# A retention recurrence followed by a two-layer MLP on one core: four small changes of order and of loading, made together

## The chip, the core and the metric

The kernel runs on one core of a Trainium2 chip. The core has five engines, each with its own instruction stream and each executing it in order: PE (TensorE, matrix products; its weight loads are shown as PEld), DVE (VectorE), ACT (ScalarE), POOL (GpSimd) and SP (SyncE, which here only issues DMA transfers). An instruction waits on semaphores for what it needs from other engines or from a transfer. The metric is the device time of one execution in microseconds.

## The reference

The first half is a linear-attention recurrence with decay over 768 positions, for 4 batches and 8 heads of width 64. The second half takes its output as 3072 tokens of width 512 and runs them through a two-layer network with a leaky activation.

```python
for t in range(S):                                   # S = 768, D = 64
    state = gamma * state + outer(k[:, :, t], v[:, :, t])
    y[:, :, t] = scale * (q[:, :, t] @ state)
x = y.transpose(0, 2, 1, 3).reshape(3072, 512)
h = x @ w_in                                         # 512 -> 2048
g = max(h, 0) + alpha * min(h, 0)
out = g @ w_out                                      # 2048 -> 512
```

## The kernel before

The tokens are worked in six blocks of 512 (`n` from 0 to 5). A block is four chunks of 128 positions. For each chunk the recurrence is computed in its chunked form: scores of the chunk (`sca`, `scb`), masked by DVE, products with v, and a state carried from chunk to chunk (`sta`, `stb`, `ss`, `t`). The first eight chunks are worked as four units of 256 positions (functions that begin with `u`), the others one by one or in pairs. The results of two chunks stand in two PSUM banks, `ya` and `yb`, one for each half of the rows, and are passed on to the 16-bit tile `xT[n]`, which is the input of the first layer of block `n`. Where part of the result was computed ahead into banks `za`/`zb` and copied to `zs`, passing on means: in one half of the columns of a bank ACT copies (`own`), in the other DVE adds `zs` (`other`). In the kernel before, both work on `ya` first and then on `yb`, and because they read the same bank, ACT's copy waits for DVE's addition (`put_y`, line 606, for chunks; `uout_copy`, line 572, for units).

The first layer is `ffn1_half` (blocks 0 and 1, two output tiles of 256 tokens at a time), `ffn1` (rest of block 0, and block 2) and `ffn1_mix` (blocks 3 to 5). After each output tile ACT makes `hm` and DVE the 16-bit activation `gt`. `ffn1_mix` computes part of the layer with seven products of quarter matrices in place of eight (a Strassen-Winograd form). It needs four sums and differences of quarters of w_in, `wins` 0 to 3 (`win_sum`, made once, on POOL, during block 2), and four of quarters of `xT`, `xsum` 0 to 3 (`x_sum`, two on DVE and two on POOL, for each block).

The second layer is `ffn2` (block 0) and `seven` (blocks 1 to 5), again seven products, of quarters of `gt` and w_out. `seven` needs sums of quarters of `gt`: `g_sums(n, part, which, engine)` makes for half `part` of the groups the sum `which`: 0 is `gs` 0 (sum of two quarters of `gt`), 1 is `gs` 1 (`gs` 0 minus a quarter), 2 is `third`, 3 changes `gt` itself. With `part` None both halves are made by one instruction. The first two products of `seven` use `gt`, the third uses `gs` 1.

Everything is in one written order: the position of a call in the program sets where its instructions stand in the streams of their engines. `tick(gen, m)` issues `m` matrix products of a layer between other calls.

The inputs come in through a ring of twelve 512 KB staging buffers (`ring`), and all loads are issued by SP in order. The first of four column pieces of w_in is loaded by `load_first` as two halves of 256 columns, each with all four row groups `j`; the other pieces by `load_w` as two halves of two row groups each, all 512 columns. POOL and ACT cast them to 16 bits (`cast_first`, `cast_w`).

Of the kernel before, what the change touches and what calls it, by code (L numbers as in the profile page):

```python
# [11 lines left out]
COPY = mybir.ActivationFunctionType.Copy  # L12
# [7 lines left out]
def kernel(  # L20
# [10 lines left out]
    nc = tc.nc  # L31
# [285 lines left out]
    def out_second(us):  # L317
        if us[0] not in zs:
            out_states(us, 1)
        z = zs.pop(us[0], None)  # L320
        yv, _ = ys.pop(us[0])
        nb, at = divmod(us[0], UB)
        if at == 0:
            xT[nb] = sbp.tile([128, 2, NP, TB // 2], F16, tag="xT", bufs=2, name=f"xT{nb}")
        to = xT[nb][:, at // 2].rearrange("p a (t x j) -> p a t x j", x=2, j=64)
        for X in range(2):
            put_y(to[:, :, :, X, :], yv[X], X, z and z[X])

    ustaged, ukq, ukT, uv, um = {}, {}, {}, {}, {}

# [242 lines left out]
    def uout_copy(w, shared=False, z=None):  # L573
        y = uy.pop(w)[0]
        nb, at = divmod(2 * w, UB)
        if at == 0:
            xT[nb] = sbp.tile([128, 2, NP, TB // 2], F16, tag="xT", bufs=2, name=f"xT{nb}")
        for X in range(2):
            lo = C * X
            to = xT[nb][:, at // 2, :, lo : lo + C].rearrange("p a (n j) -> p a j n", j=2)  # L580
            src = y[X].rearrange("p (a j n) -> p a j n", j=2, n=64)
            if z and z[X]:
                own, other = slice(2 * X, 2 * X + 2), slice(2 - 2 * X, 4 - 2 * X)
                nc.vector.tensor_tensor(out=to[:, other], in0=src[:, other], in1=z[X], op=ADD)  # L584
                nc.scalar.activation(
                    out=to[:, own], in_=src[:, own], func=COPY, bias=0.0, scale=1.0
                )
            elif shared and X == 0:
# [14 lines left out]
        nc.scalar.activation(out=t, in_=b[:, 0:256], func=COPY, bias=0.0, scale=1.0)  # L603
        return t

    def put_y(to, src, X, z):
        if z is None:
            nc.scalar.activation(out=to, in_=src, func=COPY, bias=0.0, scale=1.0)
            return
        own, other = slice(2 * X, 2 * X + 2), slice(2 - 2 * X, 4 - 2 * X)  # L610
        nc.vector.tensor_tensor(out=to[:, other], in0=src[:, other], in1=z, op=ADD)
        nc.scalar.activation(out=to[:, own], in_=src[:, own], func=COPY, bias=0.0, scale=1.0)

    gts = {}

# [436 lines left out]
    def load_w(nm, i, parts=2):  # L1052
        n = 4 // parts
        for j in (0, 2):
            t = ring(f"{nm}{i}{j}").rearrange("p (j d) -> p j d", j=2)
            if nm == "wi":
                src = wi[:, j : j + 2, 512 * i : 512 * i + 512]
            else:
                src = wo[:, 4 * i + j : 4 * i + j + 2, :]
            for jj in range(0, 2, n):  # L1060
                nc.sync.dma_start(out=t[:, jj : jj + n], in_=src[:, jj : jj + n])
            for jj in range(2):
                wst[nm, i, j + jj] = t[:, jj]
# [9 lines left out]
                eng.tensor_copy(out=to, in_=t)  # L1073


    def load_first():
        for c in range(2):
            t = ring(f"wi0{c}").rearrange("p (j d) -> p j d", j=4)
            nc.sync.dma_start(out=t, in_=wi[:, :, 256 * c : 256 * c + 256])
            wst["first", c] = t  # L1080

    def cast_first(c, engs):
        t = wst.pop(("first", c))
        for j, eng in zip(range(4), engs):
            to = w_in_all[:, j, 256 * c : 256 * c + 256]
            if eng is nc.scalar:
                eng.activation(out=to, in_=t[:, j], func=COPY, bias=0.0, scale=1.0)
            else:
                eng.tensor_copy(out=to, in_=t[:, j])
# [184 lines left out]
    for n in range(1, NBLK):  # L1274
        more = n + 1 < NBLK
        u0 = UB * (n + 1)
        if n == 2:
# [46 lines left out]
        if more:  # L1324
# [122 lines left out]
```

## Time and profile before

| | |
|---|---|
| median of three runs | 197.99 us (lowest 197.58) |
| the profiled execution's own time | 198.98 us |
| its span, first to last instruction | 197.0 us, so 1.98 us lie around it |
| PE busy | 189.3 us, 96% of the span |
| DVE, ACT, POOL busy | 151.3, 121.7 and 147.5 us |
| granted TensorE clock | 1.0 throughout |
| DMA | 38.78 MB, mean 197 GB/s |

A row of the timeline has the start, the duration, the engine, the line of the kernel, the operation, output<-inputs with the shape, and a count; a bracket at its end names the idle time before it and what ended it. Durations of a single instruction overlap a little with the next one, since engines begin an instruction before the last one has left them. A row of the chain has start, duration and what the chain went through in that time: "SPq" is SP's queue, "DMA" a transfer under way.

### The profile page before, as it was taken

How to read it: one execution, taken by the hardware profiler on the slowest of the kernel's cores; microseconds unless marked ns; L12 is line 12 of the kernel's file. 1: busy time of each engine (PE TensorE's matmuls, PEld its weight loads, DVE VectorE, ACT ScalarE, POOL GpSimd, SP SyncE). 2: the span in 40 equal slices, each digit the busy share in tenths (PEclk: the TensorE clock that was granted, in tenths of full speed). 3: DMA queues.
4: the chain of work that ended last, by engine and by line, in shares of the span. 5: the costliest groups of instructions: out<-in, count | busy, mean ns of one | idle time of the engine just before them, and what ended most of it. 6: DMA issues, size and time to landing. Idle time of an engine off the chain costs nothing.

```text
span 197.0 us, 6461 instructions
## 1 busy us (share of the span) xinstructions
PE 189.3 (96%) x2668; PEld 131.7 (67%) x2668; DVE 151.3 (77%) x260; ACT 121.7 (62%) x272; POOL 147.5 (75%) x148
## 2 busy tenths in 40 slices
PE   7789899999999989999999999999999999999993
PEld 5657444557768878744688754788754888654882
DVE  2597889253999698588897879968879977799943
ACT  3368664349687863476458988749987433687120
POOL 3286788999996955999659999579999397589000
PEclk9999999999999999999999999999999999999999
DMA  6999999999999989899999999993890011200014
GB/s 168 310 336 350 404 396 296 332 358 179 210 230 148 214 257 272 196 215 299 196 231 228 226 185 265 237 221 93 113 263 2 3 57 63 100 3 0 2 57 160
DMA packets 92749, 38.78 MB, mean 197 GB/s; under 512 B 70176, under 2 KB 88624, under 8 KB 92720
## 3 DMA queue, kind: packets, MB, share of 16 engines
q1 hardware_dynamic: 91440, 37.36, 77.2%
q10 hardware_dynamic: 1280, 1.01, 1.5%
q8 instruction: 21, 0.34, 0.7%
q14 instruction: 8, 0.07, 0.1%
HBM read 27.35 MB, written 6.29 MB: 171 GB/s over the span
## 4 chain that ended last, share of the span: by engine, by line
PE 73%; SPq 10%; DMA 7%; POOL 6%; DVE 1%; issue 1%; POOLq 0%
PE ops L809 30%; PE hps L942 16%; PE hps L632 12%; PE hps L972 5%; SPq L340 4%; SPq L117 4%; DMA wi<-in_moe_w_in_dram 4%; PE ops L734 4%; POOL wsum L757 3%; DMA kqs<-in_q_dram 3%; PE ya L293 1%; PE yb L293 1%; POOL gs L757 1%; DVE gs L757 1%; POOL ukq L354 1%; PE sca L234 1%
## 5 line engine op out<-in xcount | busy, mean ns | idle before, releaser
L809 PEld LDWEIGHTS <-gt 128*128 128x128 f16 x320 | 30.6, 98 | 4.2
L942 PE MATMUL hps<-xT,win 128*128 128x512 f16 x144 | 33.0, 379 | 0.0
L929 DVE SCALAR_TENSOR_TENSOR gt<-hm,small,hps 128x512 f16<-128x512 f32 (+1 forms) x42 | 28.7, 706 | 5.1 <-ACT hm L925 3.8
L809 PE MATMUL ops<-wout,gt 128*128 128x256 f16 x240 | 28.4, 273 | 0.0
L925 ACT ACTIVATE hm<-hps 128x512 f32<-128x512 f32 x39 | 23.1, 593 | 6.1 <-PE hps L942 5.4
L632 PE MATMUL hps<-xT,win 128*128 128x512 f16 x112 | 24.7, 379 | 0.6 <-POOL win L1073 0.6
L137 POOL TENSOR_TENSOR kq<-kqs,tab 128x512 f16<-128x512 f32 x23 | 23.7, 1051 | 1.9 <-DMA kqs<-in_q_dram 1.9
L642 DVE SCALAR_TENSOR_TENSOR gt<-hm,small,hps 128x512 f16<-128x512 f32 x28 | 20.9, 748 | 3.8 <-ACT hm L641 0.9
L942 PEld LDWEIGHTS <-win 128*128 128x128 f16 x144 | 14.1, 98 | 14.5
L641 ACT ACTIVATE hm<-hps 128x512 f32<-128x512 f32 x28 | 16.7, 597 | 8.9 <-PE hps L632 8.6
L674 DVE SCALAR_TENSOR_TENSOR gt<-hm,small,hps 128x256 f16<-128x256 f32 x40 | 16.9, 476 | 5.0 <-ACT hm L669 5.0
L827 ACT ACTIVATE kept<-ops 128x512 f32<-128x512 f32 x15 | 9.0, 597 | 18.8 <-PE ops L809 18.7
L632 PEld LDWEIGHTS <-win 128*128 128x128 f16 x112 | 10.9, 98 | 13.6 <-POOL win L1073 1.1
L809 PE MATMUL ops<-wsum,gs 128*128 128x256 f16 x160 | 19.0, 273 | 0.7 <-DVE gs L757 0.7
L217 POOL TENSOR_TENSOR t<-ss,tab 128x256 f16<-128x256 f32 x13 | 8.7, 669 | 13.6 <-DVE ss L215 13.6
L757 POOL TENSOR_TENSOR gt<-gt,gs 128x1024 f16<-128x1024 f16 x8 | 17.0, 2126 | 2.2 <-DVE gs L757 2.2
L660 PE MATMUL hps<-xT,win 128*128 128x256 f16 x160 | 18.4, 273 | 0.0
L129 ACT ACTIVATE kq<-kqs,tab 128x64 f16<-128x64 f32 x72 | 18.0, 336 | 0.0
L660 PEld LDWEIGHTS <-win 128*128 128x128 f16 x160 | 15.4, 98 | 2.6 <-DVE xT L584 0.3
L809 PEld LDWEIGHTS <-gs 128*128 128x128 f16 x160 | 15.1, 98 | 3.0 <-DVE gs L757 1.0
L669 ACT ACTIVATE hm<-hps 128x512 f32<-128x512 f32 x20 | 11.8, 597 | 4.5 <-PE hps L660 4.4
L839 DVE TENSOR_TENSOR os<-ops,kept 128x512 f32<-128x512 f32 (+1 forms) x17 | 10.5, 624 | 5.0 <-ACT kept L827 3.7
(139 smaller groups left out, 391.5 us busy)
## 6 DMA issues: line engine op xcount, KB each, us to landing
out_dram<-os SPq DMA_DIRECT2D x20, 256.0 KB, 3.6
wi<-in_moe_w_in_dram SPq DMA_DIRECT2D x8, 512.0 KB, 8.6
wo<-in_moe_w_out_dram SPq DMA_DIRECT2D x8, 512.0 KB, 8.7
kqs<-in_k_dram SPq DMA_DIRECT2D x16, 256.0 KB, 4.4
kqs<-in_q_dram SPq DMA_DIRECT2D x16, 256.0 KB, 4.3
vs<-in_v_dram SPq DMA_DIRECT2D x16, 256.0 KB, 4.7
ku<-in_k_dram SPq DMA_DIRECT2D x4, 256.0 KB, 4.4
qu<-in_q_dram SPq DMA_DIRECT2D x4, 256.0 KB, 5.3
```

Source lines behind the costliest of these rows:

```text
L129: eng.activation(out=kqs[u][:, a, h % 4, h // 4, :], in_=staged[u][nm][:, h, :], func=COPY, bias=0.0, scale=tab[:, H * a + h : H * a + h + 1],
L137: eng.tensor_tensor(out=kqs[u][:, a].rearrange("p i r d -> p r i d"), in0=staged[u][nm].rearrange("p (r i) d -> p r i d", i=4), in1=tab[:, ...
L632: nc.tensor.matmul(out=hps, lhsT=w_in_all[:, hp, 128 * ft : 128 * ft + 128], rhs=xT[n][:, :, hp, :], start=(hp == 0), stop=(hp == 3),)
L641: nc.scalar.activation(out=hm, in_=hps, func=RELU, bias=0.0, scale=-1.0)
L642: nc.vector.scalar_tensor_tensor(out=gt_at(n, ft, slice(0, TB)), in0=hm, scalar=oma_sb[:, ft : ft + 1], in1=hps, op0=MULT, op1=ADD,)
L660: nc.tensor.matmul(out=hps[:, 256 * (ft - f0) : 256 * (ft - f0) + 256], lhsT=w_in_all[:, hp, 128 * ft : 128 * ft + 128], rhs=xT[n][:, half ...
L674: nc.vector.scalar_tensor_tensor(out=gt_at(n, f, to), in0=hm[:, at], scalar=oma_sb[:, f : f + 1], in1=hps[:, at], op0=MULT, op1=ADD,)
L757: eng.tensor_tensor(out=out, in0=a, in1=b, op=op)
L809: nc.tensor.matmul(out=bk[:, 256 * t : 256 * t + 256], lhsT=a[:, f, 128 * t : 128 * t + 128], rhs=w[:, f, :], start=first and f == 0 and ( ...
L925: nc.scalar.activation(out=t, in_=src, func=RELU, bias=0.0, scale=-1.0)
L929: nc.vector.scalar_tensor_tensor(out=gt_at(n, f, cols), in0=hm, scalar=oma_sb[:, f : f + 1], in1=src, op0=MULT, op1=ADD,)
L942: nc.tensor.matmul(out=hps, lhsT=w_in_all[:, hp, 128 * ft : 128 * ft + 128], rhs=x[:, :, hp, :], start=(hp == 0), stop=(hp == 3),)
```

## The change

Four edits, made together.

1. The second piece of w_in (columns 512 to 1023) is loaded and cast like the first: as two halves of 256 columns with all four row groups (`load_columns(1)`, `cast_columns(2)` and `(3)`). POOL casts six tiles of 256 columns in place of three of 512. ACT casts two of 256 in place of one of 512, the second of them after the first output tile of `ffn1(0, lo=4)`.
2. Passing on (`put_crossed`): DVE begins on `ya` as before and ACT on `yb`; then they change banks.
3. In block 1 the three group sums on DVE are made in the order (1, 0), (0, 1), (1, 1) in place of (0, 1), (1, 0), (1, 1).
4. `win_sum(3)` on POOL moves from the end of block 2's first layer to after the `x_sum` calls for block 3.

```diff
+        put = [(to[:, :, :, X, :], yv[X]) for X in range(2)]
+        if z:
+            put_crossed(put, z)
+            return
...
+    def put_crossed(put, z):
+        own, other = [slice(0, 2), slice(2, 4)], [slice(2, 4), slice(0, 2)]
+
+        def add(X):
+            to, src = [a[:, other[X]] for a in put[X]]
+            nc.vector.tensor_tensor(out=to, in0=src, in1=z[X], op=ADD)
+
+        def copy(X, at):
+            to, src = [a[:, at] for a in put[X]]
             nc.scalar.activation(out=to, in_=src, func=COPY, bias=0.0, scale=1.0)
...
+        if z[0] is not None:
+            add(0)
+        copy(1, own[1])
+        copy(0, slice(0, 4) if z[0] is None else own[0])
+        add(1)
...
-    load_first()
-    load_w("wi", 1)
+    load_columns(0)
+    load_columns(1)
     load_w("wi", 2)
...
-    cast_first(0, [A, G, G, G])
-    cast_first(1, [A, G, A, G])
-    cast_w("wi", 1, [G, G, G])
+    cast_columns(0, [A, G, G, G])
+    cast_columns(1, [A, G, A, G])
+    cast_columns(2, [G, G, G])
+    cast_columns(3, [G, G, G])
...
             if half and f:
-                cast_w("wi", 1, [A])
+                cast_columns(2, [A], [3])
...
-    for _ in ffn1(0, lo=4):
+    gen = ffn1(0, lo=4)
+    tick(gen, 4)
+    cast_columns(3, [A], [3])
+    for _ in gen:
         pass
...
-            for i in range(4):
+            for i in range(3):
                 win_sum(i, G)
...
-            ((0, 1), (1, 0), (1, 1)) if n == 1 else ((None, 0), (None, 1)) if more else ((1, 0), (1, 1))
+            ((1, 0), (0, 1), (1, 1)) if n == 1 else ((None, 0), (None, 1)) if more else ((1, 0), (1, 1))
...
                 x_sum(n + 1, 3, G)
+                if n == 2:
+                    win_sum(3, G)
```

DVE's instructions around block 1's group sums, before. The `gs` row with `gt` alone is sum (1, 0); the two with `gs` and `gt` are (0, 1) and (1, 1); sum (0, 0) is made by POOL.

```order
L674 SCALAR_TENSOR_TENSOR gt_992<-hm,small,hps 128x256 x18
L757 TENSOR_TENSOR gs_1356<-gs_1355,gt_992 128x1024
L757 TENSOR_TENSOR gs_1355<-gt_992 128x1024
L757 TENSOR_TENSOR gs_1356<-gs_1355,gt_992 128x1024
L839 TENSOR_TENSOR os<-ops,kept 128x512
```

The same place now (the edit has moved the line numbers):

```order
L686 SCALAR_TENSOR_TENSOR gt_996<-hm,small,hps 128x256 x18
L769 TENSOR_TENSOR gs_1359<-gt_996 128x1024
L769 TENSOR_TENSOR gs_1360<-gs_1359,gt_996 128x1024 x2
L851 TENSOR_TENSOR os<-ops,kept 128x512
L203 TENSOR_TENSOR t_8_1542<-ut_4_1054,sta 128x256
```

Sum (1, 0) now stands right behind the last activation of the first layer, and the two that make `gs` 1 follow it.

POOL's instructions from the end of block 2 into block 3's first layer, before (`t` is the decayed state, `kq` a scaled k or q, `hm` and `gt` the end of a Winograd part):

```order
L217 TENSOR_TENSOR t_16_2413<-ss_2411,tab 128x256
L757 TENSOR_TENSOR xsum<-xT_2358 128x512
L757 TENSOR_TENSOR xsum<-xT_2358,xsum 128x512
L137 TENSOR_TENSOR kq_2566<-kqs_2019,tab 128x2x4x64 x2
L1002 TENSOR_TENSOR hm<-hm,small 128x512
L1008 TENSOR_TENSOR gt_2597<-hm,kept 128x2x256
```

The same place now:

```order
L217 TENSOR_TENSOR t_16_2416<-ss_2414,tab 128x256
L769 TENSOR_TENSOR xsum<-xT_2361 128x512
L769 TENSOR_TENSOR xsum<-xT_2361,xsum 128x512
L769 TENSOR_TENSOR wins<-win,wins 128x512
L137 TENSOR_TENSOR kq_2570<-kqs_2023,tab 128x2x4x64 x2
L1014 TENSOR_TENSOR hm<-hm,small 128x512
L1020 TENSOR_TENSOR gt_2601<-hm,kept 128x2x256
```

`wins` 3 stands between `xsum` 3 and the two `kq`; in front of the `t` rows of block 2 it is gone.

ACT's instructions at the end of block 2's recurrence, before:

```order
L603 ACTIVATE zs<-za 128x256
L603 ACTIVATE zs<-zb 128x256
L612 ACTIVATE xT_2358<-ya 128x4x64
L612 ACTIVATE xT_2358<-yb 128x4x64
L129 ACTIVATE kq_2389<-kqs_2014,tab 128x64 x8
L985 ACTIVATE kept<-hps 128x512
```

The same place now:

```order
L606 ACTIVATE zs<-za 128x256
L606 ACTIVATE zs<-zb 128x256
L618 ACTIVATE xT_2361<-yb 128x4x64
L618 ACTIVATE xT_2361<-ya 128x4x64
L129 ACTIVATE kq_2392<-kqs_2018,tab 128x64 x8
L997 ACTIVATE kept<-hps 128x512
```

The two copies have changed places; `kept` is the copy that frees a bank for the next Winograd part. The copy from `yb` waits for PE alone, the copy from `ya` for DVE's addition on `ya`, and DVE's addition on `yb` for ACT's copy from `yb`. The streams of PE hold the same products in the same order, and SP's the same transfers but for the shape of the two of edit 1.

More of the change, by code (lines that the diff above doesn't have):

```diff
@@ L325, in out_second @@
         to = xT[nb][:, at // 2].rearrange("p a (t x j) -> p a t x j", x=2, j=64)
-        for X in range(2):
-            put_y(to[:, :, :, X, :], yv[X], X, z and z[X])
+        put = [(to[:, :, :, X, :], yv[X]) for X in range(2)]
+        if z:
+            put_crossed(put, z)
+            return
+        for x, y in put:
+            nc.scalar.activation(out=x, in_=y, func=COPY, bias=0.0, scale=1.0)
     ustaged, ukq, ukT, uv, um = {}, {}, {}, {}, {}
@@ L577, in uout_copy @@
             xT[nb] = sbp.tile([128, 2, NP, TB // 2], F16, tag="xT", bufs=2, name=f"xT{nb}")
+        put = []
         for X in range(2):
@@ L580, in uout_copy @@
             to = xT[nb][:, at // 2, :, lo : lo + C].rearrange("p a (n j) -> p a j n", j=2)
[L581 to L588, printed above, removed]
+            put.append((to, y[X].rearrange("p (a j n) -> p a j n", j=2, n=64)))
+        if z:
+            put_crossed(put, z)
+            return
+        for X, (to, src) in enumerate(put):
+            if shared and X == 0:
                 nc.vector.tensor_copy(out=to, in_=src)
@@ L604, in z_copy @@
         return t
-    def put_y(to, src, X, z):
-        if z is None:
-            nc.scalar.activation(out=to, in_=src, func=COPY, bias=0.0, scale=1.0)
[L609 to L612, printed above, removed]
+    def put_crossed(put, z):
[5 more added lines that the diff above has]
+            to, src = [a[:, at] for a in put[X]]
+            nc.scalar.activation(out=to, in_=src, func=COPY, bias=0.0, scale=1.0)
+        if z[0] is not None:
[3 more added lines that the diff above has]
+        add(1)
     gts = {}
@@ L1073, in cast_w, with load_columns, cast_columns @@
                 eng.tensor_copy(out=to, in_=t)
-    def load_first():
-        for c in range(2):
+    def load_columns(i):
+        for c in range(2 * i, 2 * i + 2):
             t = ring(f"wi0{c}").rearrange("p (j d) -> p j d", j=4)
             nc.sync.dma_start(out=t, in_=wi[:, :, 256 * c : 256 * c + 256])
[L1080 to L1084, printed above, removed]
+            wst["columns", c] = t
+    def cast_columns(c, engs, js=range(4)):
+        t = wst["columns", c]
+        for j, eng in zip(js, engs):
             to = w_in_all[:, j, 256 * c : 256 * c + 256]
```

## The prediction

> **What bounds the kernel now.** First the page's summary of the chain of waits, then the chain's own rows ahead of 70 us:
>
> ```profile
> PE 73%; SPq 10%; DMA 7%; POOL 6%; DVE 1%; issue 1%; POOLq 0%
> ```
>
> ```profile
> 55.55 5.82 DMA kqs<-in_q_dram
> 61.44 1.04 POOL kq L137
> 62.49 4.17 POOL wsum L757 x2
> 66.65 2.09 POOL gs L757
> ```
>
> PE carries most of it, and all of it behind 71 us but for the last store. Ahead of that the chain leaves PE: SP's queue, a landing, POOL, then DVE set when block 1's second layer goes on. PE's timeline next, where it stands still, at 21 us (`ffn1` of block 0) and at 70 us (`seven` of block 1, third product):
>
> ```profile
> 20.55 0.59 PE L632 MATMUL hps<-xT,win 128*128 128x512 f16 x2
> 21.75 10.10 PE L632 MATMUL hps<-xT,win 128*128 128x512 f16 x46 [0.60 <-POOL win L1073]
> ```
>
> ```profile
> 69.56 0.60 PE L809 MATMUL ops<-wsum,gs 128*128 128x256 f16 x4
> 70.84 3.23 PE L809 MATMUL ops<-wsum,gs 128*128 128x256 f16 x28 [0.68 <-DVE gs L757]
> ```
>
> Matrix products overlap, so a wait is read from starts. One of 512 columns takes 10.10/46 = 0.22 us, one of 256 columns 3.23/28 = 0.115. At 21 the third product should have begun at 20.55 + 0.44 = 20.99 and began 0.76 later. At 70 the fifth should have begun at 69.56 + 0.46 = 70.02 and began 0.82 later. A third loss is in no list of waits, but in PE's timeline of blocks 4 and 3, where the first layer's Winograd parts come eight products at a time:
>
> ```profile
> 139.32 1.04 PE L972 MATMUL hps<-xT,win 128*128 128x256 f16 x8
> 140.19 1.03 PE L942 MATMUL hps<-xT,win 128*128 128x512 f16 x4
> 141.06 1.20 PE L972 MATMUL hps<-xsum,wins 128*128 128x256 f16 x8
> ```
>
> ```profile
> 112.42 1.18 PE L972 MATMUL hps<-xsum,wins 128*128 128x256 f16 x8
> ```
>
> The first eight take 1.04, the second eight 1.20 and 1.18: 0.16 and 0.14 are lost in them.
>
> One behaviour decides this case. POOL and DVE at the start of block 5:
>
> ```profile
> 167.95 1.15 POOL L757 TENSOR_TENSOR xsum<-xT 128x512 f16<-128x512 f16 x1 [1.90 <-ACT xT L612]
> ```
>
> ```profile
> 167.58 0.42 DVE L757 TENSOR_TENSOR xsum<-xT 128x512 f16<-128x512 f16 x1
> 168.11 1.28 DVE L757 TENSOR_TENSOR xsum<-xT,xsum 128x512 f16<-128x512 f16 x1
> ```
>
> DVE's second sum has the size of the first and takes 1.28 us in place of 0.42. POOL's sum runs until 169.10 and DVE's ends at 169.39: it stood until POOL was through and then needed 0.29, so 0.13 of its own time had passed in the wait. Here a DVE sum of two SBUF operands waits for a POOL sum that already runs. The Trainium skill (SBUF — State Buffer, "Who interferes with whom") says so: a VectorE instruction with two SBUF inputs contends with a GpSimd one that reads SBUF, the first has the port for its whole instruction, and the other is blocked.
>
> **Edit 1, w_in by columns.** POOL's casts before, the first piece's and then two of the second's:
>
> ```profile
> 15.20 2.13 POOL L1089 CAST win<-wi 128x256 f16<-128x256 f32 x5
> 18.95 1.17 POOL L1073 CAST win<-wi 128x512 f16<-128x512 f32 x2 [1.62 <-DMA wi<-in_moe_w_in_dram]
> ```
>
> Six casts of 2.13/5 = 0.43 replace three of 1.17/2 = 0.59: 0.8 us more on POOL. The first two output tiles now need only the first transfer, whose landing ended POOL's wait at 18.95, so the stall at 21 can go, up to 0.76. But POOL is through with this piece up to 0.8 later, and PE wants the third piece 0.76 earlier, so most of the stall can also come back four tiles on. Neither end reaches the end of the program: up to 70.02 PE has 0.82 in hand, and what it waits for there comes by loads and POOL. I cost both at nothing; the cover is this 0.82. Without it the edit would be worth the 0.76.
>
> What does reach the end is a shift of the loads, since that chain hangs on a landing. The DMA rates (the last two columns are DMA share and GB/s; the five before the clock are engines) with 1 KB packets, with 2 KB ones, and where the one gives way to the other:
>
> ```profile
> 14.00:15.00 1.00, 0.91 (x75) 0.79 (x68) 1.00 (x3) 0.94 (x2) 0.92 (x2) 1.00 1.04 360
> 18.00:19.00 1.00, 1.00 (x11) 0.90 (x10) 0.24 (x1) 0.60 (x1) 0.05 (x1) 1.00 1.04 404
> 15.50:17.00 1.50, 1.13 (x32) 0.64 (x31) 1.29 (x4) 1.50 (x5) 1.50 (x5) 1.00 0.92 275
> ```
>
> 1.05 MB at 360 in place of 404 GB/s take 2.92 - 2.60 = 0.32 us more, and all later loads land that much later. Where the packets change, the rate falls to 275, which costs 1.5 x (404 - 275)/404 = 0.48; if that belonged to this piece alone and went with it, the loads would gain 0.16. Between -0.16 and +0.32 I take **+0.10**, near the middle, as no row tells the two apart. The Trainium skill (DMA: Bandwidth & Descriptors, "Specifications") gives 512 B as the least transfer for line rate; by it the shift would be 0 and the sum below smaller by 0.10. The rows, 360 against 404, do not bear it out here.
>
> **Edit 3, block 1's order.** POOL's sum (0, 0) and DVE's three:
>
> ```profile
> 66.61 2.12 POOL L757 TENSOR_TENSOR gs<-gt 128x1024 f16<-128x1024 f16 x1
> ```
>
> ```profile
> 68.77 0.69 DVE L757 TENSOR_TENSOR gs<-gs,gt 128x1024 f16<-128x1024 f16 x1 [1.69 <-POOL gs L757]
> 69.38 0.68 DVE L757 TENSOR_TENSOR gs<-gt 128x1024 f16<-128x1024 f16 x1
> 70.09 0.69 DVE L757 TENSOR_TENSOR gs<-gs,gt 128x1024 f16<-128x1024 f16 x1
> ```
>
> DVE is free at 68.77 - 1.69 = 67.08. If (1, 0) ran at once, the last sum would follow (0, 1) at 69.38 and end at 70.07 in place of 70.78: 0.71 gained. But POOL's sum runs from 66.61 to 68.73 and (1, 0) has two SBUF operands, so it ends at 68.73 + 0.68 - 0.13 = 69.28. Then (0, 1) begins 0.07 ahead of that, as consecutive sums do in these rows, and (1, 1) 0.61 after it, at 69.82, to end at 70.51: 0.27 earlier. PE's first four products need (0, 1) at 69.90 and are through at 70.42, in time. If DVE comes first because PE is early, POOL's sum is the blocked one, and the total stays. I take **-0.27**, between -0.71 and 0.
>
> **Edit 2, passing on.** Block 4's input: ACT, DVE's sum behind it, and PE's weight load:
>
> ```profile
> 138.50 0.38 ACT L612 ACTIVATE xT<-ya 128x256 f16<-128x256 f32 x1 [0.23 <-DVE xT L611]
> 138.84 0.38 ACT L612 ACTIVATE xT<-yb 128x256 f16<-128x256 f32 x1
> 139.12 2.01 ACT L129 ACTIVATE kq<-kqs,tab 128x64 f16<-128x64 f32 x8
> 141.03 0.58 ACT L985 ACTIVATE kept<-hps 128x512 f32<-128x512 f32 x1
> ```
>
> ```profile
> 138.92 1.14 DVE L757 TENSOR_TENSOR xsum<-xT 128x512 f16<-128x512 f16 x1
> ```
>
> ```profile
> 141.65 0.31 PEld L972 LDWEIGHTS <-wins 128*128 128x128 f16 x3 [0.17 <-issue]
> ```
>
> ACT waits 0.23 for DVE, copies twice and scales; its `kept` copy ends at 141.61 and PE goes on at 141.65, which is the 0.16. Now ACT copies `yb` in that wait and is through 0.23 to 0.34 earlier, `kept` too, so the 0.16 goes, and in block 3 the 0.14. DVE's second addition comes later by part of a copy, but the sum behind it took 1.14 in place of 0.42, so it stood 0.72 for POOL anyway. In blocks 1 and 2 PE does not stand for `xT`. Worth up to **-0.30**, or 0 if PE waits there for something else.
>
> **Edit 4, `wins` 3.** POOL where it was and where it goes; then DVE, then PE:
>
> ```profile
> 95.52 1.16 POOL L757 TENSOR_TENSOR wins<-win,wins 128x512 f16<-128x512 f16 x1
> 100.58 0.61 POOL L217 TENSOR_TENSOR t<-ss,tab 128x256 f16<-128x256 f32 x1 [3.90 <-DVE ss L215]
> ...
> 114.71 2.05 POOL L137 TENSOR_TENSOR kq<-kqs,tab 128x512 f16<-128x512 f32 x2
> ...
> 123.89 2.13 POOL L757 TENSOR_TENSOR third<-gt 128x1024 f16<-128x1024 f16 x1
> ```
>
> ```profile
> 125.92 1.23 DVE L757 TENSOR_TENSOR gs<-gt 128x2048 f16<-128x2048 f16 x1
> 127.18 1.23 DVE L757 TENSOR_TENSOR gs<-gs,gt 128x2048 f16<-128x2048 f16 x1
> ```
>
> ```profile
> 128.48 3.22 PE L809 MATMUL ops<-wsum,gs 128*128 128x256 f16 x28
> ```
>
> It leaves a place behind which POOL idles 3.90 us: nothing gained. It enters at 114.71, where POOL goes without a pause to 123.89. All that follows moves by its 1.16, less the 0.04 by which instructions overlap: 1.12. That is the two `kq`, with the transpose and twelve loads queued behind them on SP (wanted a block later, so free); three pairs of `hm` and `gt`, the last of which is then through at 125.0; and `third`, 125.01 to 127.14. DVE still finds its `gt` at 125.92, but now meets `third` running: it ends at 127.14 + 1.23 - 0.13 = 128.24, and `gs` 1, 0.03 behind it, at 129.50 in place of 128.41. PE began on `gs` 1 at 128.48, only 0.07 after it was there. So PE stands **+1.09**; without the block the edit costs 0. By the Trainium skill's wording (the same section) a blocked instruction has its whole length still to go; that would add 0.13, and the 0.29 above speaks against it. Block 3's 0.14 from edit 2 is swallowed here, since POOL does not follow PE.
>
> Sum: +0.10 - 0.27 - 0.16 + 1.09 = **+0.76**. The profiled execution, 198.98 with a span of 197.0, would take 199.74; from the median of 197.99 it is 198.8.
>
> **Rivals.** *No blocking in either place*: the long DVE sums waited for something else, and edits 2 and 3 give all they can: +0.10 - 0.71 - 0.30 = -0.91, 197.1, faster than before. For it: POOL's spans are rough. Against it: 0.42 and 1.28 for the same work. Chance 0.12.
>
> *Blocking is real, but `third` misses DVE's sum*: +0.10 - 0.27 - 0.30 = -0.47, 197.5. `third` would have to come less than about 0.2 late, or over 2.0. The rows put it at 1.12, right between. Chance 0.18.
>
> *Edit 1 does not do what it says*: the halves land no earlier, and PE waits at 21 as before. With 0.82 in hand at 70 the time is that of the forecast, in whose chance it is counted.
>
> *Slower still*: loads late by the full 0.32 and no gain in block 1, +0.32 - 0.16 + 1.09 = +1.25, 199.2. It decides where the 275 GB/s stretch comes again behind this piece. Chance 0.10.
>
> **How the numbers follow.** The forecast has 0.60. Its own range is 198.3 to 199.3: 0.26 below and 0.22 above for the loads, 0.27 above and below for block 1, not all at once. The two runs shown lie 0.4 apart. The range of 8 in 10 takes in the slower rival with that scatter, 199.6, and on the other side reaches the first rival's edge, 197.0. Two per cent, 3.96 us, is about what a measurement of this kernel can tell from no change. No case comes near it: faster 0.01, same 0.97, slower 0.02.
>
> **What would show it.** Edit 1: the 46 products at 21 us without their bracket, but PE still waiting for DVE's `gs` near 70. Edit 3: DVE's (1, 0) near 2 us long and the last sum's end near 70.5; if (1, 0) takes 0.7 beside POOL's sum, blocking is wrong here. Edit 2: the second eight L972 products of block 4 in 1.04. Edit 4: DVE's first `gs` of block 3 over 2 us long and PE idle about 1.1 us ahead of its `gs` products; if it takes 1.23, the forecast falls to 197.5.

## The result, and the profile after

The changed kernel takes 199.76 us (median of 22 runs) against 198.19 for the kernel before (22 runs beside them): the ratio is 1.008, 95% interval 1.0051 to 1.0109, so 1.0 to 2.2 us slower. That is within 2%, in the direction forecast, and about twice the forecast 0.76; 199.76 lies 0.16 above the range.

Three more comparisons were made, each on one chip with its own runs of before:

| comparison | changed, median (runs) | before, median (runs) | ratio, 95% interval |
|---|---|---|---|
| first | 199.76 (22) | 198.19 (22) | 1.0080, 1.0051–1.0109 |
| second (all4_again) | 199.95 (12) | 198.91 (35) | 1.0080, 1.0045–1.0116 |
| third (all4_third) | 199.38 (13) | 199.11 (35) | 1.0014, 0.9982–1.0045 |
| fourth (all4_fourth) | 200.97 (6) | 198.31 (29) | 1.0119, 1.0067–1.0170 |

The ratios leave disturbed executions out, so they differ a little from the quotients of the medians; and since the first profile of the changed kernel was of such an execution, the lines below are from the second's (span 198.3).

Its chain of waits, by engine, and the part of the chain's rows ahead of the first stretch that PE runs alone:

```profile
PE 83%; DMA 6%; POOL 2%; DVE 2%; SPq 2%; issue 1%; ACT 1%
```

```profile
41.07 1.38 POOL ukq L358 x2
43.05 2.05 POOL ukq L358 x2
45.12 7.01 DMA ukT<-ukq
```

Before, the chain left PE last near 70 us, over a landing, POOL's `wsum` and `gs`. Now it leaves PE near 52, over the transpose of the keys that SP issues behind the loads, and then only once more before the last store, for 2.5 us ahead of block 3's `gs` products. PE's timeline at the two places of the prediction and at this one:

```profile
20.84 10.52 PE L644 MATMUL hps<-xT,win 128*128 128x512 f16 x48
...
52.27 0.24 PE L487 MATMUL sca<-ukT 64*64 64x128 f16 x2 [1.34 <-DMA ukT<-ukq]
...
70.08 3.66 PE L821 MATMUL ops<-wsum,gs 128*128 128x256 f16 x32
```

The first layer at 21 us runs as one group of 48 without a bracket: the stall is gone. But 1.34 us are lost at 52, and near 70, where PE had stood 0.82, it does not stand at all.

Edit 2 in blocks 3 and 4 (PE), where the second eight took 1.18 and 1.20:

```profile
112.12 1.04 PE L984 MATMUL hps<-xsum,wins 128*128 128x256 f16 x8
...
141.63 1.04 PE L984 MATMUL hps<-xsum,wins 128*128 128x256 f16 x8
```

Edit 3 in block 1: POOL's sum (0, 0), then DVE's (1, 0) and the two behind it:

```profile
66.11 2.13 POOL L769 TENSOR_TENSOR gs<-gt 128x1024 f16<-128x1024 f16 x1
```

```profile
67.63 1.15 DVE L769 TENSOR_TENSOR gs<-gt 128x1024 f16<-128x1024 f16 x1
68.70 1.28 DVE L769 TENSOR_TENSOR gs<-gs,gt 128x1024 f16<-128x1024 f16 x2
```

DVE came to (1, 0) only 1.52 us after POOL had begun, so it stood for a shorter time than was forecast; it ended at 68.78, 0.54 after POOL's sum, where the prediction's rule gives 0.68 - 0.13 = 0.55. The last sum was through at 69.98, before PE came to it.

Edit 4 in block 3: POOL, then DVE, then PE:

```profile
114.22 1.16 POOL L769 TENSOR_TENSOR wins<-win,wins 128x512 f16<-128x512 f16 x1
...
124.52 2.12 POOL L769 TENSOR_TENSOR third<-gt 128x1024 f16<-128x1024 f16 x1
```

```profile
125.48 2.24 DVE L769 TENSOR_TENSOR gs<-gt 128x2048 f16<-128x2048 f16 x1
127.76 1.22 DVE L769 TENSOR_TENSOR gs<-gs,gt 128x2048 f16<-128x2048 f16 x1
```

```profile
124.54 3.67 PE L821 MATMUL ops<-wout,gt 128*128 128x256 f16 x32
129.04 3.23 PE L821 MATMUL ops<-wsum,gs 128*128 128x256 f16 x28 [0.83 <-ACT kq L129]
```

`third` runs until 126.64, DVE's first sum ends 1.08 later at 127.72 and took 2.24 in place of 1.23. From the start of the 32 products to the `gs` products it is 4.50 us; before it was 128.48 - 124.98 = 3.50, with no wait. So PE stands 1.00. (The bracket names ACT's `kq`; that is only the last event the profile has ahead of it. What came last is DVE's second sum, which ended at 128.98, 0.06 earlier.)

### The profile page after: what moved, and what is told of

Same layout as the page of the kernel before. It is cut to its first block, busy times and chain, and to the rows that moved or that the text cites. A ratio compares the mean times of both kernels' runs of the same rounds, so it can differ in the third digit from the quotient of the medians.

```text
span 200.7 us, 6459 instructions
## 1 busy us (share of the span) xinstructions
PE 188.1 (94%) x2668; PEld 130.6 (65%) x2668; DVE 152.3 (76%) x260; ACT 121.5 (61%) x273; POOL 147.9 (74%) x151
## 4 chain that ended last, share of the span: by engine, by line
PE 68%; DMA 17%; SPq 6%; POOL 3%; DVE 2%; issue 1%; ACT 0%; DVEq 0%
PE ops L821 29%; PE hps L954 15%; DMA wo<-in_moe_w_out_dram 8%; PE hps L644 7%; DMA wi<-in_moe_w_in_dram 5%; PE hps L984 5%; SPq L344 5%; PE hps L672 4%; DMA ukT<-ukq 4%; DVE gs L769 2%; POOL ukq L358 2%; PE ops L708 2%; PE ya L293 1%; POOL wout L1085 1%; SPq L1091 1%; PE yb L293 1%
## 5 line engine op out<-in xcount | busy, mean ns | idle before, releaser
L654 DVE SCALAR_TENSOR_TENSOR gt<-hm,small,hps 128x512 f16<-128x512 f32 x28 | 20.9, 748 | 4.1 <-ACT hm L653 1.4
```

Of the source, the lines that this page charges most:

```text
L654: nc.vector.scalar_tensor_tensor(out=gt_at(n, ft, slice(0, TB)), in0=hm, scalar=oma_sb[:, ft : ft + 1], in1=hps, op0=MULT, op1=ADD,)
```

## The experiments

Single executions of one kernel differ by several us (the 35 of before on the second chip took 196.77 to 202.78), so each profile is read in two parts, from two rows of PE's timeline: the start of block 2's `gs` products (called the front) and from there to the start of block 5's (the rest). In the kernel before, profiled again, and in the changed one they are

```profile
99.48 1.25 PE L809 MATMUL ops<-wsum,gs 128*128 128x256 f16 x10
...
185.05 3.66 PE L809 MATMUL ops<-wsum,gs 128*128 128x256 f16 x32
```

```profile
99.28 1.47 PE L821 MATMUL ops<-wsum,gs 128*128 128x256 f16 x12
...
185.45 3.66 PE L821 MATMUL ops<-wsum,gs 128*128 128x256 f16 x32
```

so 99.48 and 85.57, 99.28 and 86.17. "Block 3" is the stand before its `gs` products, start to start, less the 3.50 above. All in us:

| kernel | front | rest | block 3 |
|---|---|---|---|
| before, two profiles | 99.78, 99.48 | 85.26, 85.57 | 0, 0 |
| before with block 3's `third` on DVE | 98.75 | 85.52 | 0 |
| before with PE's code shifted | 99.73 | 85.17 | 0 |
| edit 1 alone | 98.09 | 86.39 (0.84 of it a wait of `yb` for no cause the profile shows) | 0 |
| edit 2 alone | 98.70 | 85.08 | 0.08 |
| edit 3 alone | 98.56 | 85.36 | 0 |
| edit 4 alone | 102.69 | 86.31 | 0.71 |
| edits 2, 3 | 101.09 | 85.04 | 0.08 |
| edits 1, 2, 3, two profiles | 97.81, 100.60 | 86.04 (0.96 of it such a wait, of `third` products), 85.11 | 0, 0 |
| edits 2, 3, 4 | 98.54 | 86.17 | 1.20 |
| all four, four profiles | 101.69, 99.28, 101.97, 100.88 | 86.15, 86.17, 86.17, 86.15 | 1.27, 1.00, 1.29, 1.13 |
| all four, block 3's `third` on DVE, two | 99.24, 98.81 | 85.54, 85.52 | 0, 0 |

The rest tells the kernels apart, to a tenth where PE does not stand without cause (the two profiles of before differ by 0.3, all of it in block 2's second layer, where the second has such a wait near 106). The front does not: it runs from 97.8 to 102.7, and each kernel that was profiled twice or more has a spread of its own there.

**The whole, on the second chip.** The changed kernel, nothing undone.

> The changed kernel, unaltered, for a profile to set beside the one of before. Theory A (edit 4 as predicted, 1.1 us, and edit 1 makes every later load land late, which reaches the product on the sums of block 1's second layer): 1.3 to 1.9 us above before; the loads behind w_in's second piece land 0.5 to 1 us later than in the profile of before, PE stands 1.0 to 1.1 us before block 3's gs products, and block 1's gs products begin later than 70.84 us. Rival B (the prediction's sum is right and the difference of 0.8 us is scatter between runs): 0.5 to 1.0 us above, loads at most 0.3 us later. Rival C (edit 4 costs about 2 us, edits 1 to 3 what was predicted): 1.3 to 1.9 us above, PE stands about 2 us in block 3, loads at most 0.3 us later.

Ratio 1.008. The profile is the one shown above: PE stands 1.00 in block 3, not 2 (against C). Block 1's `gs` products begin at 70.08, not later than before (against the second half of A). The pieces of w_in come no later either: the last of the eight lands at 25.83, before at 25.89, and the median from issue to landing of its eight loads, in before and then here, is

```profile
wi<-in_moe_w_in_dram SPq DMA_DIRECT2D x8, 512.0 KB, 8.6
```

```profile
wi<-in_moe_w_in_dram SPq DMA_DIRECT2D x8, 512.0 KB, 8.5
```

**Edits 1, 2 and 3 without edit 4.**

```diff
-            for i in range(3):
+            for i in range(4):
                 win_sum(i, G)
...
-                if n == 2:
-                    win_sum(3, G)
```

> The changed kernel with w_in's last difference back in its old place, so edits 1, 2 and 3 alone. Theory A: 0.2 to 0.8 us above before (about 1.1 us below the changed kernel). Rival B: 0.3 us below before. Rival C: 0.2 to 0.5 us below before. In all three DVE's two gs sums of block 3 take 1.23 us each again and PE does not stand before its gs products.

199.46 against 198.91, ratio 1.0054 (1.0012–1.0097), 0.2 to 1.9 us: what A gave, and somewhat more by the ratio. PE did not stand in block 3, as all three had it. The profile does not show A's late loads, though: its span is 196.7 and its front 97.81, both below before's. So this comparison spoke for A, and its own profile against; it was made again below.

**Edit 1 alone.** The kernel before with w_in's second piece loaded and cast by columns.

```diff
-    load_w("wi", 1)
+    load_columns(1)
...
-    cast_w("wi", 1, [G, G, G])
+    cast_columns(2, [G, G, G])
+    cast_columns(3, [G, G, G])
```

> The kernel before with edit 1 alone: w_in's second piece loaded and cast by columns. Theory A: 0.6 to 1.2 us slower than before; the loads behind that piece land 0.5 to 1 us later and PE's goods for block 1's second layer come that much later. Rivals B and C: 0.0 to 0.3 us slower, loads later by 0.1 to 0.3 us. The 0.76 us stall of PE at 21 us is gone in all, or is found at the third piece instead.

199.30 against 198.91, ratio 1.0045 (1.0010–1.0080), 0.2 to 1.6 us, which leaves room for A and for B and C. The landings speak against A: from the first landing of w_in to the sixth, the end of its third piece, it is 6.6 to 7.7 us in the nine profiles of kernels with edit 1 (mean 7.0) and 6.8 to 8.2 in the nine without it (mean 7.4). No stall at 21 us. Of the nine with edit 1 none has that stall, though one waits 0.33 for POOL's cast four tiles on, near 26, as the prediction thought possible; of the nine without it six have it, of 0.2 to 0.76, in the mean over the nine 0.3. Yet the front is 99.8 in the mean with edit 1 and 99.7 without: what is saved at 21 is not there at 100.

**Edits 2 and 3 alone.**

```diff
+        if z[0] is not None:
+            add(0)
+        copy(1, own[1])
+        copy(0, slice(0, 4) if z[0] is None else own[0])
+        add(1)
...
-            ((0, 1), (1, 0), (1, 1)) if n == 1
+            ((1, 0), (0, 1), (1, 1)) if n == 1
```

> The kernel before with edits 2 and 3 alone: the passing on begun on different banks, and block 1's sums in the new order. By the prediction's terms 0.27 + 0.16 + 0.14 = 0.57 us faster than before, as block 3's 0.14 is not swallowed without edit 4: all theories here give 0.3 to 0.6 us faster. A rival D, in which edit 2 or 3 costs something that the trace did not show (DVE's second addition later, POOL's sum the blocked one), gives 0 to 0.5 us slower.

199.78 against 198.91, ratio 1.006 (1.0018–1.0102): a miss for the common forecast, and more than D's. D's place was not found: the rest is the shortest of all (85.04), and the time went in the front. The largest of PE's waits in its one profile there is in block 1's first layer, at products that both orders have alike:

```profile
49.65 3.65 PE L672 MATMUL hps<-xT,win 128*128 128x256 f16 x32 [1.22 <-ACT ut L450]
```

**The kernel before against itself.**

> The kernel before, unaltered: what a comparison of a kernel with itself gives, and a second profile of it. Theory E (the 0.82 us that PE stood at 70 us belongs to that one execution): PE stands at most 0.3 us before block 1's gs products, so edit 3 had nothing to gain in an ordinary execution; the comparison gives within 0.3 us of no change. Rival F (the 0.82 us is there in every execution): 0.6 to 0.9 us of standing there again. Beside it, theory C (code): where PE stands for nothing that the profile shows, it is at its 1217th, 449th, 3009th or 4033rd instruction, 256 or a multiple of it apart, where a new block of its code begins.

Ratio 0.9997 (0.9952–1.0043). PE and DVE near 70 us:

```profile
69.48 0.60 PE L809 MATMUL ops<-wsum,gs 128*128 128x256 f16 x4
70.37 3.23 PE L809 MATMUL ops<-wsum,gs 128*128 128x256 f16 x28 [0.29 <-DVE gs L757]
```

The fifth product should have begun at 69.48 + 0.46 = 69.94 and began 0.43 later, where the prediction's profile had 0.82: between E and F. In the profile of edit 1 alone, which has DVE's old order too, there is nothing:

```profile
68.73 3.66 PE L809 MATMUL ops<-wsum,gs 128*128 128x256 f16 x32
```

Of the seven profiles with DVE's old order only these two have the wait; in the other five it is 0.1 at most. So this wait belongs to the execution, not to the kernel: in the prediction's profile the chain reaches it over a landing and POOL, and it is there or not with when PE and the landing come.

**Edit 2 alone, edit 3 alone.** The first half of the diff above, then the second.

> The kernel before with edit 2 alone, the passing on begun on different banks. By the prediction 0.30 us faster (0.16 in block 4, 0.14 in block 3): the second eight of the Winograd products take 1.04 us in both blocks. Theory E the same. Rival D (edit 2 is what made edits 2 and 3 together slow, by DVE's later addition): 0.5 to 1.0 us slower, with PE standing for xT or for a sum of xT somewhere in blocks 1 to 5.

198.92 against 198.80, ratio 1.0006 (0.9973–1.0040); the second eight take 1.04 in both blocks, and the rest is 85.08, the best of the single edits. The 0.3 is in the profile; in the comparison it is lost in the scatter. The interval (0.5 below to 0.8 above) would leave room for D, but the profile has no stand for `xT` or its sums, so D is out for edit 2.

> The kernel before with edit 3 alone, block 1's sums in the new order. By the prediction 0.27 us faster. Theory E: no change, within 0.2 us, as PE does not wait for these sums in an ordinary execution. Rival D (DVE's first sum is blocked by POOL's and delays what stands behind it on DVE): 0.3 to 0.9 us slower, with PE standing before block 1's gs products longer than in the kernel before.

198.66 against 198.80, ratio 1.0017 (0.9971–1.0064), 0.6 below to 1.3 above: no change that can be told, as E had it, and PE does not stand before block 1's `gs` products, against D. Neither edit alone is seen to be slow, and behind the front the two together are the fastest of all; the 0.9 us above is left to the front, its cause open.

Edit 3 has the other branch that the prediction named. POOL and DVE in the second profile of edits 1, 2, 3:

```profile
67.71 2.59 POOL L769 TENSOR_TENSOR gs<-gt 128x1024 f16<-128x1024 f16 x1
```

```profile
67.62 0.69 DVE L769 TENSOR_TENSOR gs<-gt 128x1024 f16<-128x1024 f16 x1
70.33 1.29 DVE L769 TENSOR_TENSOR gs<-gs,gt 128x1024 f16<-128x1024 f16 x2 [2.02 <-POOL gs L769]
```

Here DVE came first, took its ordinary 0.69, and POOL's sum was the longer one, 2.59 for 2.12. Whoever starts first has its own time; the other pays. The two sums that need POOL's come the later for it, and PE waited 0.84 for them at 71.07: in this execution the wait near 70 is there with the new order.

**Edit 4 alone.** The kernel before with `win_sum(3, G)` moved.

> The kernel before with edit 4 alone, w_in's last difference moved from POOL's stretch near 95 us to the one near 115 us. By the prediction and theory E 1.09 us slower: POOL's third part of block 3 runs beside DVE's first gs sum, which takes over 2 us, and PE stands 0.8 to 1.1 us before its gs products. Rival G (it costs less, since block 3's own slack covers part): 0.3 to 0.6 us slower with PE standing as long as that.

199.41 against 198.80, ratio 1.0040 (1.0004–1.0076), 0.1 to 1.5 us. Block 3, DVE then PE:

```profile
129.15 1.95 DVE L757 TENSOR_TENSOR gs<-gt 128x2048 f16<-128x2048 f16 x1
131.13 1.23 DVE L757 TENSOR_TENSOR gs<-gs,gt 128x2048 f16<-128x2048 f16 x1
```

```profile
128.21 3.67 PE L809 MATMUL ops<-wout,gt 128*128 128x256 f16 x32
132.42 2.79 PE L809 MATMUL ops<-wsum,gs 128*128 128x256 f16 x24 [0.54 <-DVE gs L757]
```

Alone, PE stands 132.42 - 128.21 - 3.50 = 0.71; with edit 2, 1.00 to 1.29. The price is steadier than the stand. In all six profiles with edit 4 and POOL's `third`, this one too, `third` ends 27.33 to 27.36 us after the front, where both profiles of before have 26.2, and the `gs` products begin 29.73 to 29.76 after it, before 28.70 and 29.00. So POOL sets this stretch: what PE gains on the way, as edit 2's 0.14, only makes it stand longer, and what it loses, as 0.3 in block 2, comes off the stand.

**Taking edit 4's price away.** All four edits, but DVE makes the first part of block 3's `third` behind its `gs` sums, so that POOL's no longer runs beside them.

```diff
-            if s == 15:
+            if s == 15 and n != 3:
                 g_sums(n, 0, 2 if n + 1 < NBLK else 0, nc.gpsimd)
...
             g_sums(n, p, w, V)
+        if n == 3:
+            g_sums(n, 0, 2, V)
```

> The changed kernel, but block 3's first part of the third sum is made by DVE behind its two gs sums instead of by POOL beside them. If edit 4's price is POOL's third blocking DVE's gs (the prediction): both gs sums of block 3 take 1.23 us again, PE does not stand before its gs products (at most 0.1 us), and the time is 0.8 to 1.1 us below the unaltered changed kernel on the same chip. Rival H (POOL's 1.12 us of delay reach PE another way, through gt or kq): PE still stands 0.5 us or more there, and the time is within 0.3 us of the changed kernel.

198.14, against 199.38 for the changed kernel on the same chip, 1.24 less, and 199.11 before (ratio 0.9955, 0.9922–0.9988). DVE, then PE:

```profile
125.53 1.23 DVE L769 TENSOR_TENSOR gs<-gt 128x2048 f16<-128x2048 f16 x1
126.78 1.22 DVE L769 TENSOR_TENSOR gs<-gs,gt 128x2048 f16<-128x2048 f16 x1
```

```profile
124.58 3.67 PE L821 MATMUL ops<-wout,gt 128*128 128x256 f16 x32
128.08 3.51 PE L821 MATMUL ops<-wsum,gs 128*128 128x256 f16 x28
```

`wins` 3 still stands on POOL where edit 4 put it, and POOL is as late as before; only the meeting of the two sums is gone, and with it the whole stand. That shows the price and its mechanism, and H is out. Behind the front the gain is smaller than the stand, 86.17 to 85.54: DVE's `third` makes the stretch from block 3's `gs` products (128.08 here) to its last sixteen (136.69) 8.61 us in place of 8.33, and a loss of 0.3 in block 2 no longer comes off a stand. The other 0.6 of the 1.24 would then lie in the front, which this edit does not touch.

**Without edit 1, and the whole beside it.** Edits 2, 3 and 4, with `load_w("wi", 1)` and its casts as before; then all four.

> Edits 2, 3 and 4 without edit 1. Theory E (ahead of 70 us PE follows the loads, so the stall at 21 us is worth nothing): within 0.4 us of the changed kernel. Rival J (edit 1 gains its 0.4 us of stall in the mean): 0.3 to 0.8 us above the changed kernel. Rival A (edit 1 makes the loads late): 0.4 us or more below the changed kernel, and the third piece of w_in lands 0.3 us or more earlier after the first piece than with edit 1.

> The changed kernel, unaltered, on the same chip as the three others: 0.8 to 1.4 us above before, PE standing 0.8 to 1.1 us before block 3's gs products; the 46 products of the first layer at 21 us without a stall; and, by theory E, no wait of 0.3 us or more for DVE's gs near 70 us, but one for the transposed keys near 52 us where the loads are late.

199.31 and 199.38: edit 1 is worth 0.1 us here by the medians, with a scatter of some 0.4, as E had it. By the ratios to before, 1.0058 (1.0015–1.0101) and 1.0014, it would be worth 0.9, about what J had; the intervals overlap, so the times do not decide, and edit 1 alone had come out slower. Block 3 has its stand in both (1.20 and 1.29). Near 52 us PE waited 1.13 for the keys without edit 1,

```profile
51.52 0.24 PE L487 MATMUL sca<-ukT 64*64 64x128 f16 x2 [1.13 <-DMA ukT<-ukq]
```

so that wait is not edit 1's doing; in the whole's profile here, where PE had waited 2.59 near 18, it is not there. The whole was only 0.27 above before on this chip, less than was expected.

**The versions without the price, once more on one chip.** The same edits as above; in the third the diff on `third` is put on the kernel before.

> Edits 1, 2 and 3 without edit 4, once more. If edits 1 to 3 gain what the traces show behind 70 us and nothing ahead of it (0.3 us in blocks 3 and 4): 0 to 0.5 us below before, and within 0.3 us of the kernel with block 3's third on DVE. If the earlier 1.1 us above before was theirs: 0.6 us or more above before.

> All four edits with block 3's first third on DVE, once more. If edits 1 to 3 gain as above: 0 to 0.5 us below before. If the 0.9 us below before was theirs and the earlier 1.1 us above was chance: 0.6 us or more below before, and edits 1 to 3 without edit 4 the same.

> The kernel before with block 3's first third on DVE, none of the four edits. In the profile of before POOL's third ends before DVE's first gs sum of block 3 begins, so nothing is blocked there and nothing can be gained: within 0.2 us of before. If the change gains something by itself (POOL freed for what stands behind it): 0.4 us or more below before.

> The changed kernel once more. By the prediction's terms without edit 3's 0.27 (as PE was seen to wait near 70 us in only some executions): 0.7 to 1.1 us above before, and 1.0 to 1.2 us above both versions without edit 4's price.

Before 198.31; edits 1 to 3 198.20 (0.9990, 0.9952–1.0028); all four with `third` on DVE 198.27 (0.9979, 0.9942–1.0015); before with `third` on DVE 198.70 (1.0014, 0.9979–1.0049); the whole 200.97 (1.0119, 1.0067–1.0170). Edits 1 to 3 are here between 0.9 below and 0.6 above; the earlier comparison had them 0.2 to 1.9 above, so the times do not fix what they are worth, and the rest gives 0.15 (85.11 against 85.26). `third` on DVE gains nothing by itself; it costs 0.29 in block 3's second layer here too. (In the profile of before POOL's third did not end before DVE's sum began, as this expectation has it, but 0.10 after, at 126.02 against 125.92; a meeting so short cost DVE nothing, 1.23 us as without it.) The whole came out 2.7 above, more than expected; its profile shows where one execution lost so much, and it is in the front (last section).

**PE's code shifted.** The kernel before with 16 throwaway products more.

```diff
-    busy(2, tag="pb")
+    busy(2, tag="pb", small=8)
...
-    busy(2, tag="pb")
+    busy(2, tag="pb", small=8)
```

> The kernel before with 16 throwaway products of 64 columns more at 10 to 12 us, where PE waits for data: 32 PE instructions, so that every later block of 256 of PE's code begins 32 instructions earlier in the program. Theory C (PE stands where a new block of its code has not come yet): the waits without a cause are at the 449th, 1217th, 3009th instruction of this kernel's own count, which are other products than before; where PE runs 256 instructions in 2.2 to 2.7 us (two places, near 104 and 163 us) it stands 0.5 to 2 us, and the time is 1 to 4 us above before. Rival K (these waits belong to the products, not to the count): they stay at the same products, and the time is within 0.5 us of before.

198.63 against 199.11, ratio 0.9992 (0.9950–1.0034). C's price is wrong: at the two places with 256 instructions in 2.2 to 2.7 us PE did not stand. Of the old products only that near 15.5 us, the 449th of before, still waited: 0.5 us, for POOL's `uv` by the profile, as K had it. At the 1217th and 3009th there was no wait by either count, so this execution does not tell the two theories apart there.

## Why the prediction was right and wrong, point by point

**Edit 4: right, with its size.** Forecast 1.09 with edit 2's gain swallowed; PE's stand was 1.00 to 1.29 in five profiles with edits 2 and 4, DVE's first sum took over 2 us in each, and the stand went when the meeting was taken away. POOL's delay is right as well: `third` ends 1.1 later against the front than in before, where 1.12 was forecast. That a blocked sum has done part of its own time holds too: in the second profile 125.48 to 127.72 with `third` ending at 126.64, so 1.08 after the release where the rule gave 1.23 - 0.13 = 1.10. It is 1.08 in all eight profiles in which DVE was held up there.

**Edit 2: right.** 1.04 at both places. Block 4's 0.16 is kept; block 3's 0.14 is swallowed by POOL, as forecast.

**The two together.** Behind the front the forecast was 1.09 - 0.16 = 0.93. The rest is 86.16 for the whole and 85.26 and 85.57 for before: 0.6 to 0.9. The 0.3 between the two is the wait of before's second profile in block 2; such a loss lengthens before, but not the whole, where POOL sets that stretch.

**Edit 1: its own stall went, and the cover was wrong.** The prediction costed it at nothing since PE had 0.82 us in hand at 70. In most executions it does not have them there. What lies between and can take the gain is the keys' transpose at 52 (1.34 in one profile, 1.13 in another), PE's waits near 16 and 48 us that depend on the execution, and what is left of the wait at 70; which of them did, no run isolates. The result, no gain that the runs can tell, is near the forecast by luck; the reason is not the one given. The loads' shift of 0.10 does not show: 8.6 and 8.5 us from issue to landing, and the third piece lands no later after the first. The Trainium skill (DMA: Bandwidth & Descriptors, "Specifications") has line rate from 512 B on, so no shift; on the loads the runs agree with it, and the rates 360 and 404 were two stretches of one execution.

**Edit 3: the step that failed.** The blocking was right (DVE's (1, 0) ends 0.54 after POOL's sum, forecast 0.55), but the gain "I take -0.27" takes it that PE waits for these sums, and this was read from one wait of 0.82 us in one execution. (By starts it is 0.84: these products begin 0.11 apart, not 0.115, since 3.23/28 takes in the whole length of the last one.) A second profile of the same kernel has 0.43, and the five others with the same order 0.1 at most; none of the four profiles of the whole has it. Edit 3 alone changed the time by -0.14 in the medians and +0.3 in the ratio, with an interval that holds -0.27 as well, so it is the profiles that speak against the term. Without it the prediction's sum is +1.03, inside the measured 1.0 to 2.2; the rest of the distance to 1.57 is not accounted for by any term.

**The range: too narrow for the same reason.** It allowed for 0.4 us of scatter, the distance of two runs of before, and the 198.19 of before in the comparison already lies 0.20 above the 197.99 that it starts from. Single executions scatter by a standard deviation of 1.3 us (91 runs of before), and the profiles put it in the front, 97.8 to 102.7. Between two medians of 22 runs that alone leaves some 0.4 us.

**What stays open.** 0.6 to 0.9 us behind the front are shown. The four comparisons, weighted by their scatter, give some 1.2 us with an uncertainty of 0.2 (a standard error, from 1.57, 1.04, 0.27 and 2.66 with 1.3 us for one run); the third and the fourth lie over twice their own scatter from 1.2, so the true uncertainty is larger. Whether the front of the whole is really slower by 0.3 to 0.6 us, or chance, the runs do not tell: over all profiles with and without edit 1 it is equal within 0.1, but four profiles of the whole have 101.0 in the mean, and two with `third` on DVE, the same up to there, 99.0. A halved clock (last section) is in two of those four, at 101.97 and 100.88, but not in the one at 101.69.

## What to carry to other kernels

Moving a sum to another place on POOL is priced by what it then meets, not by the gap it fills: look for the VectorE sum with two SBUF operands that it, or what it delays, will run beside (here 1.1 us of delay were enough). A wait in one profile is a sample: before an edit is credited with removing it, take a second profile of the same kernel, and see whether the wait is there. And where executions scatter more than the edit is worth, compare profiles by stretches between two fixed products: here the rest repeated to 0.02 us in four executions while the whole spans differed by 2.7.

## What the runs showed of the hardware

**Waits at every 256th instruction of PE.** The waits of PE that the profiles of the unshifted kernels put down to nothing ("issue") are at the 449th, 1217th, 2241st, 3009th or 4033rd of its 5,350 instructions in the trace: 193 plus a multiple of 256. Three of them, the first the longest:

```profile
18.11 0.22 PE L427 MATMUL stb<-uv,ukq 64*64 64x64 f16 x2 [2.59 <-issue]
```

```profile
105.19 0.27 PE L821 MATMUL ops<-wsum,third 128*128 128x256 f16 x1 [0.81 <-issue]
```

```profile
47.77 3.65 PE L660 MATMUL hps<-xT,win 128*128 128x256 f16 x32 [0.22 <-issue]
```

They are from the third comparison's profile of the whole, from edits 1 to 3 and from edit 3 alone. The last is at the 1217th, and so is the wait of 1.22 at 49.65 above, which the profile puts down to ACT's `ut`; in ten of the seventeen profiles of unshifted code that product waited 0.3 us at most. PE's code comes by a queue of its own, 21 packets of 16 KB in all (first line; 5,350/256 is 20.9); the one for the second of the three waits began between 102.9 and 103.0 (second line, that stretch alone), 2.2 us before PE went on:

```profile
q8 instruction: 21, 0.34, 0.7%
```

```profile
q8 instruction: 1, 0.02, 58.6%
```

In the seventeen profiles of unshifted code PE passed none of these five places sooner than 2.2 us after the last packet ahead of it began, and that packet came 0.4 to 5.2 us after PE had passed the place 256 instructions before, latest while the loads ran. The Trainium skill (Runtime: NRT & Kernel Launch, "Instruction fetch mechanics") gives the blocks of 16 KiB, 256 instructions, which agrees, and calls the cost mostly hidden; if these waits are that cost, it was up to 2.6 us in one place here. That the waits move when the code is shifted was not seen, so the cause is argued from these numbers, not shown.

**Two waits ahead of a halved clock.** In the fourth profile of the whole PE waited 1.81 us at 46.6. The next seven products came 0.11 us apart, as usual, and then sixteen 0.21 apart. PE's row and the stretch behind it (granted clock third from the end):

```profile
48.44 5.32 PE L672 MATMUL hps<-xT,win 128*128 128x256 f16 x32 [1.81 <-ACT ut L450]
```

```profile
48.40:52.00 3.60, 3.56 (x21) 2.67 (x21) 1.23 (x4) 1.17 (x2) 3.52 (x4) 0.61 1.27 226
```

The third profile has the same behind the wait of 2.59 at 18.11 shown above:

```profile
19.79 5.26 PE L672 MATMUL hps<-xT,win 128*128 128x256 f16 x32
```

```profile
20.00:23.00 3.00, 3.00 (x16) 2.14 (x15) 1.27 (x3) 1.26 (x2) 3.00 (x7) 0.50 1.05 404
```

In both the granted clock is 0.5 for 3.41 us, from 49.2 and from 19.7. 5.32 and 5.26 in place of 3.65: another 1.67 and 1.61 on top of the waits. In the other sixteen profiles no wait behind PE's first instruction is longer than 1.49, and none has such a stretch once the clock has risen; after the wait of 1.22 in the profile of edits 2 and 3 the group took 3.65. So a wait in front can cost nearly twice its length. That the wait brings the slow clock is read from the order in time, in two cases; no run sets the length of a wait. The Trainium skill (TensorE: Matmul & The Clock Gate, "HAM oscillation — how this bites in real kernels") has the rule that gaps above about 3.4 us bring the slow clock; here gaps of 1.81 and 2.59 came ahead of it.

Much of the scatter between executions goes with this clock. 3.41 us at half speed are 0.009 of a span, and of 146 timed executions of before seven have a mean clock of 0.991, all others 0.997 or more. The seven took 201.8 us in the mean, the others 198.7. Of the whole's 53, four have 0.992 or less, 202.0 us against 199.9.
